# Decode attention on one core: the maximum of a head crosses partitions by two small TensorE products and two VectorE instructions instead of twelve VectorE instructions, and TensorE runs nine unread products meanwhile

## The chip, the cores and the metric

One core of one Trainium2 chip. The metric is device time in microseconds.

## The reference

Two attention blocks decode one token each, and their outputs are concatenated. A has 32 heads and 32 caches of 32768 keys; B has 32 heads over 8 caches, and only the last 4096 keys count. Head size is 128 and everything is bf16.

```python
# A, cut; B is the same on the last 4096 keys, four query heads to a cache
q = (x @ wq) ...                                     # 32 heads x 128
scores = einsum("bhqd,bhkd->bhqk", q, k_cache) * 128 ** -0.5
p = softmax(scores)
o = einsum("bhqk,bhkd->bhqd", p, v_cache)
return o.reshape(1, 1, 4096) @ wo
```

A's K and V are 8.39 MB each for a head, 16.78 MB together. That is what the kernel mostly does: read 570 MB once.

## The kernel before

A head of A goes like this. K (8.39 MB) and V (8.39 MB) arrive by two DMAs from one queue, in order: K of head g, V of head g, K of head g+1. The K tiles are transposed on TensorE (`psT`), copied out by VectorE (`kt`), and multiplied with the query into `psS`, 128 rows of 512 scores. Then come the maximum, the exponential on ScalarE, four transposes of the probabilities (`psPT`), and 64 products with V into `psACC` (called PV below). VectorE folds them, and TensorE gathers them into `psG`. The loop body holds two heads, and 16 trips make 32 heads.

The maximum, which the change touches. VectorE alone brings the row maxima of 128 partitions to one number and back:

```python
        o = dve(lambda v: v.reduce_max(tr["in"][:, 0:1], self.S[:, :], axis=AXX), self.sdone, self.k_pool)
        o = dve(lambda v: v.transpose(tr["a"][:, :], tr["in"][:, :]), o)
        for c in range(STRIPS):
            x = dve(lambda v, c=c: v.tensor_copy(m4[0:1, W * c:W * c + W], tr["a"][32 * c:32 * c + 1, 0:W]), o)
        o = dve(lambda v: v.reduce_max(t["mr"][0:1, :], m4[0:1, 0:4 * W].rearrange("p (k h) -> p h k", h=HG), axis=AXX), x)
        for c in range(STRIPS):
            x = dve(lambda v, c=c: v.tensor_copy(
                t["b"][32 * c:32 * c + 1, 0:W].rearrange("p (k h) -> p k h", k=KC),
                t["mr"][0:1, :].unsqueeze(1).to_broadcast([1, KC, HG])), o)
        o = dve(lambda v: v.transpose(t["cm"][:, :], t["b"][:, :]), x)
        o = dve(lambda v: v.tensor_scalar_mul(t["nb"][:, k:k + 1], t["cm"][:, 0:1], -self.SCALE), o, to="act")
        self.sread = self.op("act", lambda s: s.activation(
            out=self.psb[:, :], in_=self.S[:, :], func=ACTF.Exp, bias=t["nb"][:, k:k + 1], scale=self.SCALE,
            accum_out=t["oc"][k][:, DH:DH + 1]), o, self.psread, to="pe")
```

When buffers come free. V has one buffer, so the next V load is issued when PV of this head has ended. The next K load is issued when this head's transposes have left one part of the K buffer:

```python
    def load_v(self, g):
        self.load(self.vbuf[:, :], self.kv_src("v", "A", g)[:, 0, :], self.mark("v", 0), *self.free["v"])
    ...
        for g in range(NQH):
            self.loop = {"pe": g // 2, "dve": g // 2}
            self.load_k(g, 1 if g < NQH - 1 else 2)
            self.load_v(g)
            self.emit_qcopy(g)
            self.emit_unit("A", g)
            self.emit_stats("A", g)
            self.emit_PT("A", g)
            self.emit_PV("A", g)
```

The end. After the last head, both output matrices (`wo`) come in through the same queue, B's in two pieces and A's in four (12, 10, 6 and 4 of 32 row blocks). TensorE multiplies them as they land:

```python
    WO_CUTS = {"A": (0, 12, 22, 28, 32), "B": (0, 16, 32)}
    ...
    def emit_proj(self):

        for part in range(len(self.WO_CUTS["B"]) - 1):
            o = self.proj_part("B", part, lambda a: (self.S[32 * (a % 4):32 * (a % 4) + 1, :], (0, 32 * (a % 4)), a < 4, a >= 28))
        strips = self.op("dve", lambda v: v.tensor_copy(self.pb[:, :], self.S[:, :]), o)
        for part in range(len(self.WO_CUTS["A"]) - 1):
            last = self.proj_part("A", part, lambda a: (self.PT[0:1, :], None, a == 0, a == 31))
            if part == 0:
                o = self.op("pe", lambda e: e.matmul(self.ACC[0:1, :], lhsT=self.e32[:, 0:1], rhs=self.pb[:, :],
                                                     start=True, stop=True, skip_group_check=True), strips, self.accread)
                self.store("B", self.ACC, 512, o)
        self.store("A", self.PT, 0, last)
```

## Time and profile before

| | before |
|---|---|
| median of the first 3 runs | 1331.03 us (1330.01 to 1332.43) |
| span of the profiled run | 1330.5 us |
| bytes read | 570.4 MB |
| K of one head to K of the next | 38.7 us |
| start of the maximum to the exponential | 3.11 us |
| the 64 PV products of one head | 5.7 us |

From the page of the profile before: busy times, the granted TensorE clock and the DMA share in 40 slices (a digit is tenths), the load queue, and the chain of waits by engine.

```profile
span 1330.5 us, 28787 instructions
...
PE 953.2 (72%) x13274; PEld 668.9 (50%) x13274; DVE 805.0 (61%) x1661; ACT 54.8 (4%) x167; POOL 2.0 (0%) x15
...
PEclk9868788887788888778889878888987888888788
DMA  9999999999999999999999999999999999999997
...
q1 hardware_dynamic: 12628, 570.43, 99.4%
...
DMA 68%; PE 28%; DVE 3%; issue 0%; ACT 0%; SPq 0%
```

The transfer row stands at 9 throughout and the load queue is busy 99.4% of the span: the loads pace the program. The clock row dips in most slices, because TensorE pauses several times in each head.

One head in the timeline of before (start in us, duration in us, engine, line, operation; in brackets the idle time before and what ended it). The lines are the maximum, the exponential, PV, the issue of the next V load, and the first transposes of the next K.

```profile
610.83 0.69 DVE L522 TENSOR_REDUCE tr_in<-psS 128x1 f32<-128x512 f32 x1 [0.51 <-PE psS L505]
...
613.94 0.69 ACT L533 ACTIVATE psb<-psS,nb_A 128x512 bf16<-128x512 f32 x1 [35.86 <-DVE nb_A L532]
...
616.07 5.68 PE L571 MATMUL psACC<-vbuf,ptsb 128*4 128x512 bf16 x64 [0.69 <-ACT ptsb L546]
...
621.80 0.33 SPq L284 DMA_DIRECT2D vbuf<-in_A_v_cache_dram  x1
...
627.49 5.17 PE L483 MATMUL psT<-ident,kbuf 128*128 128x128 bf16 x64 [3.67 <-DMA kbuf<-in_A_k_cache_dram]
```

Read from top to bottom: 3.11 us from maximum to exponential, PV of 5.68 us, the next V issued at 621.80, and TensorE idle until K lands at 627.49.

The end of before: PV of head 31, B's 32 products, A's first 12, A's last 20, and the last eviction (the copy of A's result out of the accumulator).

```profile
1308.15 6.09 PE L571 MATMUL psACC<-vbuf,ptsb 128*4 128x512 bf16 x64 [0.69 <-ACT ptsb L546]
...
1317.15 3.29 PE L627 MATMUL psS<-kbuf,oz_B 128*1 128x512 bf16 x32
...
1320.27 2.75 PE L627 MATMUL psPT<-kbuf,oz_A 128*1 128x512 bf16 x12
...
1323.71 4.48 PE L627 MATMUL psPT<-kbuf,oz_A 128*1 128x512 bf16 x20
...
1328.23 0.68 DVE L633 CAST out_sb<-psPT 1x512 bf16<-1x512 f32 x1 [3.64 <-PE psPT L627]
```

No bracket here names a DMA. From K of head 30 on (first used at 1247.5 us), the program moves by computing alone.

### The profile page before, as it was taken

Reading aid. Unit: us, or ns where it says so; the run is one execution under the profiler, and the core shown is the slowest. Engines: PE = TensorE matmul, PEld = TensorE weight load, DVE = VectorE, ACT = ScalarE, POOL = GpSimd, SP = SyncE. Lnnn points to the kernel's source line nnn. Section 1 sums busy time; section 2 is a strip of 40 time slices with the busy share of each in tenths; the row PEclk is TensorE's granted clock in tenths of the full one; section 3 lists DMA queues with packets and bytes.
Section 4 is the critical chain, followed back from the end, with each engine's and each line's share of the span. In section 5 each row is a group of like instructions: output and inputs, shape, how many; then the busy total and the mean of one; then the engine's idle time right before and its main releaser. Section 6 shows DMA issues by size and latency. Waiting matters only on the chain.

```text
span 1330.5 us, 28787 instructions
## 1 busy us (share of the span) xinstructions
PE 953.2 (72%) x13274; PEld 668.9 (50%) x13274; DVE 805.0 (61%) x1661; ACT 54.8 (4%) x167; POOL 2.0 (0%) x15
## 2 busy tenths in 40 slices
PE   3756677686767778676687867668787667868777
PEld 3544445554444555444455544446554444555452
DVE  2655566765556676555667655566765556676573
ACT  0000000000000000000000000000000000000000
POOL 0000000000000000000000000000000000000000
PEclk9868788887788888778889878888987888888788
DMA  9999999999999999999999999999999999999997
GB/s 394 429 438 429 437 428 439 431 422 439 418 435 433 437 428 431 431 439 431 433 430 439 431 433 430 439 431 433 432 437 430 435 431 428 439 435 431 428 435 322
DMA packets 12932, 570.66 MB, mean 429 GB/s; under 512 B 1522, under 2 KB 1524, under 8 KB 1780
## 3 DMA queue, kind: packets, MB, share of 16 engines
q1 hardware_dynamic: 12628, 570.43, 99.4%
q8 instruction: 12, 0.20, 0.1%
q10 hardware_dynamic: 288, 0.00, 0.0%
q14 instruction: 4, 0.03, 0.0%
HBM read 570.43 MB, written 0.00 MB: 429 GB/s over the span
## 4 chain that ended last, share of the span: by engine, by line
DMA 68%; PE 28%; DVE 3%; issue 0%; ACT 0%; SPq 0%
DMA kbuf<-in_A_k_cache_dram 65%; PE psT L483 23%; PE psS L505 3%; DMA kbuf<-in_B_k_cache_dram 3%; DVE kt L486 3%; PE psACC L571 1%; PE psPT L627 1%; PE psS L627 0%; DVE oc_A L587 0%; ACT psb L533 0%; PE psPT L543 0%; DVE tr_in L522 0%; DVE b_A L528 0%; DVE m L525 0%; SPq L284 0%
## 5 line engine op out<-in xcount | busy, mean ns | idle before, releaser
L486 DVE COPY kt<-psT 128x1024 bf16<-128x1024 bf16 x1056 | 655.3, 684 | 203.0 <-PE psT L483 201.4
L483 PE MATMUL psT<-ident,kbuf 128*128 128x128 bf16 x8448 | 577.7, 234 | 135.8 <-DMA kbuf<-in_A_k_cache_dram 123.8
L483 PEld LDWEIGHTS psT<-ident,kbuf 128*128 128x128 bf16 x8448 | 538.3, 106 | 227.8 <-DMA kbuf<-in_A_k_cache_dram 131.9
L571 PE MATMUL psACC<-vbuf,ptsb 128*4 128x512 bf16 (+1 forms) x2112 | 188.5, 534 | 22.8 <-ACT ptsb L546 22.0
L505 PE MATMUL psS<-kt,qw 128*32 128x512 bf16 x2048 | 157.6, 385 | 15.5 <-DVE kt L486 15.5
L585 DVE TENSOR_SCALAR oc_A<-psACC,hot_A 128x128 f32<-128x128 f32 x32 | 11.2, 351 | 255.5 <-PE psG L598 255.5
L571 PEld LDWEIGHTS psACC<-vbuf,ptsb 128*4 128x4 bf16 (+1 forms) x2112 | 60.8, 111 | 141.9 <-issue 96.1
L543 PE MATMUL psPT<-ident,psb 128*128 128x128 bf16 x136 | 20.5, 305 | 127.9 <-ACT psb L533 127.9
L543 PEld LDWEIGHTS psPT<-ident,psb 128*128 128x128 bf16 x136 | 11.7, 130 | 137.6 <-ACT psb L533 137.4
L533 ACT ACTIVATE psb<-psS,nb_A 128x512 bf16<-128x512 f32 x32 | 22.0, 687 | 1169.7 <-DVE nb_A L532 1169.7
L505 PEld LDWEIGHTS psS<-kt,qw 128*32 128x32 bf16 x2048 | 34.0, 95 | 58.0 <-DVE kt L486 31.4
L598 PE MATMUL psG<-oc_A,hw 128*32 128x128 f32 (+1 forms) x128 | 19.3, 227 | 52.3 <-DVE oc_A L587 52.3
L598 PEld LDWEIGHTS psG<-oc_A,hw 128*32 128x32 f32 x128 | 11.4, 109 | 62.4 <-DVE oc_A L587 55.0
L587 DVE SCALAR_TENSOR_TENSOR oc_A<-psACC,hot_A,oc_A 128x128 f32<-128x128 f32 x96 | 33.7, 351 | 3.4
L522 DVE TENSOR_REDUCE tr_in<-psS 128x1 f32<-128x512 f32 x34 | 23.5, 692 | 17.1 <-PE psS L505 17.1
L525 DVE COPY m<-tr_a 1x16 f32<-1x16 f32 (+1 forms) x136 | 22.3, 164 | 2.6
L528 DVE COPY b_A<-mr_A 1x16 f32<-1x16 f32 x128 | 21.1, 165 | 2.4
L546 ACT ACTIVATE ptsb<-psPT 128x512 bf16<-128x512 bf16 x34 | 20.3, 597 | 32.3 <-PE psPT L543 32.3
L439 PE MATMUL psACC<-x_B,vbuf 128*128 128x1 bf16 x128 | 3.6, 165 | 13.4 <-DMA x_B<-in_B_x_dram 13.4
L439 PEld LDWEIGHTS psACC<-x_B,vbuf 128*128 128x128 bf16 x128 | 3.5, 104 | 13.4 <-DMA x_B<-in_B_x_dram 13.4
L446 DVE CAST qz<-psACC 128x32 bf16<-128x32 f32 x1 | 0.2, 192 | 12.9 <-PE psACC L439 12.9
L523 DVE STREAM_TRANSPOSE tr_a<-tr_in 128x32 f32<-128x32 f32 x34 | 7.2, 212 | 1.2
(66 smaller groups left out, 87.5 us busy)
## 6 DMA issues: line engine op xcount, KB each, us to landing
kbuf<-in_B_k_cache_dram SPq DMA_DIRECT2D x2, 4096.0 KB, 32.7
vbuf<-in_B_v_cache_dram SPq DMA_DIRECT2D x2, 4096.0 KB, 23.7
kbuf<-in_A_k_cache_dram SPq DMA_DIRECT2D x2, 4096.0 KB, 22.7
vbuf<-in_B_wq_dram SPq DMA_DIRECT2D x1, 4096.0 KB, 12.3
vbuf<-in_A_wq_dram SPq DMA_DIRECT2D x1, 4096.0 KB, 32.5
kbuf<-in_B_wo_dram SPq DMA_DIRECT2D x2, 2048.0 KB, 31.8
kbuf<-in_A_wo_dram SPq DMA_DIRECT2D x1, 1536.0 KB, 27.5
kbuf<-in_A_wo_dram SPq DMA_DIRECT2D x1, 1280.0 KB, 30.2
```

The costliest lines, as they stand in the source:

```text
L483: inst = e.transpose(T[:, 128 * k:128 * k + 128], src[:, DH * k:DH * k + DH], self.ident[:, :])
L486: self.copies.append(self.op("dve", lambda v: v.tensor_copy(KT[:, :], T[:, :]), o, to="pe"))
L505: inst = e.matmul(self.S[32 * c:32 * c + 32, :], lhsT=win, rhs=self.kt[(bb + c // 2) % NKT][:, 512 * (c % 2):512 * (c % 2) + 512], start=b ...
L522: o = dve(lambda v: v.reduce_max(tr["in"][:, 0:1], self.S[:, :], axis=AXX), self.sdone, self.k_pool)
L525: x = dve(lambda v, c=c: v.tensor_copy(m4[0:1, W * c:W * c + W], tr["a"][32 * c:32 * c + 1, 0:W]), o)
L528: x = dve(lambda v, c=c: v.tensor_copy(t["b"][32 * c:32 * c + 1, 0:W].rearrange("p (k h) -> p k h", k=KC), t["mr"][0:1, :].unsqueeze(1).to ...
L533: self.sread = self.op("act", lambda s: s.activation(out=self.psb[:, :], in_=self.S[:, :], func=ACTF.Exp, bias=t["nb"][:, k:k + 1], scale= ...
L543: inst = e.transpose(PT[:, 128 * jj:128 * jj + 128], self.psb[:, 128 * jj:128 * jj + 128], self.ident[:, :])
L546: self.ptread = self.op("act", lambda s: s.activation(out=self.ptsb[:, :], in_=PT[:, 0:512], func=ACTF.Copy), self.psread, to="pe")
L571: inst = e.matmul(acc[32 * c:32 * c + rows, 0:512], lhsT=lhsT, rhs=rhs, start=begin, stop=end, tile_position=(0, 32 * c), skip_group_check ...
L587: o = self.op("dve", lambda v, src=src, hot=hot: v.scalar_tensor_tensor(out=oc, in0=src, scalar=hot, in1=oc, op0=ALU.mult, op1=ALU.add), p ...
L598: return self.op("pe", lambda e: e.matmul(self.G[0:32, c0 + c:c0 + c2], lhsT=win, rhs=t["oc"][g % 2][:, c:c2], start=False, stop=True, ski ...
```

## The change

The intent is to shorten the path from scores to probabilities. After the first maximum, twelve small VectorE instructions become two products and two VectorE instructions. A product with the maxima as stationary operand lays them out along a row (`rows64` picks the right 16 of each strip), VectorE takes one maximum over 64, and a second product with a row of `-SCALE` spreads the scaled negative to 128 partitions. Nine products whose result nobody reads (`keep_busy`) are put between, so that the TensorE clock does not drop before PV. B keeps the old way.

```diff
--- before.py
+++ after.py
@@ -240,6 +240,8 @@
         self.e32 = sb("e32", [128, 32], F32)
         self.spread = sb("spread", [32, 4, 128], BF16)
         self.tr = {k: sb(f"tr_{k}", [128, 32], F32) for k in ("in", "a")}
+        self.rows64 = sb("rows64", [128, 64], F32)
+        self.nscale = sb("nscale", [1, 128], F32)
         self.m4 = sb("m4", [1, 128], F32)
         self.pb = sb("pb", [128, 512], F32)
         self.out_sb = sb("out_sb", [1, 1024], BF16)
@@ -403,6 +405,8 @@
         pool(lambda g: g.memset(self.tr["in"][:, :], 0.0))
         pool(lambda g: g.memset(self.qw[:, :], 0.0))
         pool(lambda g: g.memset(self.spread[:, :, :], 0.0))
+        pool(lambda g: g.memset(self.rows64[:, :], 0.0))
+        pool(lambda g: g.memset(self.nscale[:, :], -self.SCALE))
         for n in ("B", "A"):
             pool(lambda g, n=n: g.memset(c[n]["hsel"][:, :], 0.0))
             self.k_pool = pool(lambda g, n=n: g.memset(c[n]["b"][:, :], 0.0))
@@ -424,6 +428,10 @@
             lh = dve(lambda v, t=t, HG=HG, KC=KC: v.reduce_sum(
                 t["lh"][:, :], self.e32[:, 0:KC * HG].rearrange("p (k h) -> p h k", k=KC), axis=AXX), last)
             dve(lambda v, t=t, HG=HG: v.tensor_copy(t["hsel"][:, 32:32 + HG], t["lh"][:, :]), lh, self.k_pool)
+        for s in range(STRIPS):
+            rows = slice(32 * s, 32 * s + 32)
+            dve(lambda v, rows=rows, s=s: v.tensor_copy(self.rows64[rows, 16 * s:16 * s + 16],
+                                                        self.ident[rows, 32 * s:32 * s + 16]), self.k_pool)
         for dq in range(4):
             self.k_sel = dve(lambda v, dq=dq: v.tensor_copy(self.spread[:, dq, dq:128:4], self.ident[0:32, 0:32]),
                              self.k_pool)
@@ -519,7 +527,24 @@
         k = g % 2
         tr, m4 = self.tr, self.m4
         dve = lambda fn, *deps, **k: self.op("dve", fn, *deps, **k)
-        o = dve(lambda v: v.reduce_max(tr["in"][:, 0:1], self.S[:, :], axis=AXX), self.sdone, self.k_pool)
+        o = dve(lambda v: v.reduce_max(tr["in"][:, 0:1], self.S[:, :], axis=AXX), self.sdone, self.k_pool,
+                to="pe" if name == "A" else None)
+        if name == "A":
+
+            self.keep_busy(4)
+            o = self.op("pe", lambda e: e.matmul(self.ACC[0:1, 0:64], lhsT=tr["in"][:, 0:1], rhs=self.rows64[:, :],
+                                                 start=True, stop=True, skip_group_check=True),
+                        o, self.accread, self.k_sel, to="dve")
+            o = dve(lambda v: v.reduce_max(t["mr"][0:1, :], self.ACC[0:1, 0:64], axis=AXX), o, to="pe")
+            self.keep_busy(1)
+            o = self.op("pe", lambda e: e.matmul(self.ACC[:, 64:65], lhsT=self.nscale[:, :], rhs=t["mr"][0:1, :],
+                                                 start=True, stop=True, skip_group_check=True), o, to="dve")
+            self.keep_busy(4)
+            o = dve(lambda v: v.tensor_copy(t["nb"][:, k:k + 1], self.ACC[:, 64:65]), o, to="act")
+            self.sread = self.op("act", lambda s: s.activation(
+                out=self.psb[:, :], in_=self.S[:, :], func=ACTF.Exp, bias=t["nb"][:, k:k + 1], scale=self.SCALE,
+                accum_out=t["oc"][k][:, DH:DH + 1]), o, self.psread, to="pe")
+            return
         o = dve(lambda v: v.transpose(tr["a"][:, :], tr["in"][:, :]), o)
         for c in range(STRIPS):
             x = dve(lambda v, c=c: v.tensor_copy(m4[0:1, W * c:W * c + W], tr["a"][32 * c:32 * c + 1, 0:W]), o)
@@ -533,6 +558,16 @@
         self.sread = self.op("act", lambda s: s.activation(
             out=self.psb[:, :], in_=self.S[:, :], func=ACTF.Exp, bias=t["nb"][:, k:k + 1], scale=self.SCALE,
             accum_out=t["oc"][k][:, DH:DH + 1]), o, self.psread, to="pe")
+
+    def keep_busy(self, n):
+
+        def mm(e):
+            inst = None
+            for _ in range(n):
+                inst = e.matmul(self.PT[:, :], lhsT=self.ident[:, :], rhs=self.kt[0][:, 0:512], start=True, stop=True,
+                                skip_group_check=True)
+            return inst
+        self.op("pe", mm, self.ptread)
 
     def emit_PT(self, name, g):
         d, t = self.X[name], self.c[name]
```

## The prediction

> **What bounds the kernel now.** The loads. On the page, the transfer row of the 40 slices reads 9 everywhere but in the last, and the load queue is busy 99.4% of the span. 570.4 MB have to be read. In the middle, successive K tiles are first used at 588.8, 627.5, 666.2 and 704.9 us (chain of waits): 38.7 us for 16.78 MB, 434 GB/s. The Trainium skill, "DMA: Bandwidth & Descriptors", Specifications, gives a fabric ceiling of 435 GB/s; this trace agrees. The chain of waits is 68% DMA, 28% TensorE, 3% VectorE. The timeline of one head (600 to 640 us): TensorE ends at 623.8 and sits until 627.5, when the next K lands. The V load is issued at 621.8 but the K ahead of it lands only at 627.5, so it already queues 5.7 us; the K load issued at 637.9 lies some 9 us behind the V. The engine with slack is the computing side.
>
> **What the change does, per head of A (estimates from the timeline).** Now, from the start of the maximum over the scores (610.83) to the exponential (613.94) is 3.11 us: 0.69 maximum, then eleven small VectorE instructions of 0.15 to 0.21. Afterwards: 0.69, a product (0.27 with handoff, as the gather to the VectorE step at 621.6 shows), a maximum over 64 (0.25), a second product (0.27), a copy (0.2), and about 0.1 to 0.2 of delay from the unread products: about 1.9 us, so 1.2 us saved. VectorE loses some 1.8 us of work per head.
>
> The nine unread products cost about 2 us of TensorE (0.216 each at full clock) in time in which it is idle now (4.0 us before the transposes of the probabilities). They should keep the clock up: now it reads 0.50 from about 614 to 620, after that idle, and the 64 PV products take 5.7 us. The Trainium skill, "TensorE: Matmul & The Clock Gate", Part 1, puts the drop after an idle window of about 3.4 us; the trace agrees (two such drops per head). Warm, PV should take about 3.5 us. V is then released some 3 to 3.5 us earlier per head.
>
> **How much is on the critical path.** In 30 of 32 heads nothing: earlier release only lengthens the queue, and the TensorE wait for K grows from 4 to about 7 us. The tail is different. From 1247.5 us on, the chain is TensorE and VectorE: heads 30 and 31, then the output projections to 1328.2. There 3.5 us twice would be saved, but V of head 31 lands at 1305.6 (issue 1280.6 + 25.0) and the last piece of wo at about 1325.3 (1292.9 + 32.4), against the last product's end at 1328.2. Four products and the store remain, so at most about 2 us come off. With TensorE waiting for wo pieces in short bursts, its clock may fall and the 32 products run at 0.43 us: that could eat the gain. I expect 0.8 us.
>
> **Predicted: 1330.2 us, range 1328.2 to 1332.0.** Faster by over 2%: 0.01; within 2%: 0.98; slower by over 2%: 0.01.
>
> **Signs.** Right: the 38.7 us period and 434 GB/s unchanged; maximum to exponential about 1.9 us; the clock at 1.0 through PV, PV about 3.5 us; V issued 3 us earlier but landing at the same time, so time from issue to landing grows from 25 to about 28 us; VectorE busy down from 805 to about 747 us. Wrong: idle stretches in the transfer row, or the K period changing.
>
> **What would make it wrong.** Transfers slowing under the added reads; a hidden gap in the loads that the earlier release fills; the clock falling in the final projection, giving slightly slower; scatter between runs, which is 2.4 us in three runs already.

## The result

| | before | after |
|---|---|---|
| median, 6 runs each | 1331.85 us (1330.01 to 1332.43) | 1332.55 us (1330.07 to 1332.94) |
| ratio after / before | | 1.0004, 95% interval 0.9991 to 1.0017 |
| start of maximum to exponential | 3.11 us | 2.03 us |
| 64 PV products, mid-kernel head | 5.68 us | 3.63 us |
| VectorE busy | 805.0 us | 750.5 us |
| K of head 30 to the last eviction | 80.7 us | 82.4 us |

A ratio is the mean time of one kernel's fast runs over that of the other's in the same rounds, so it is not quite the ratio of the medians quoted.

The time did not move by an amount these runs can tell. The median of 1332.55 us lies above the predicted range (1328.2 to 1332.0). The page after, same lines as before:

```profile
span 1330.8 us, 29273 instructions
...
PE 969.7 (73%) x13658; PEld 690.4 (52%) x13690; DVE 750.5 (56%) x1345; ACT 54.8 (4%) x167; POOL 2.3 (0%) x17
...
PEclk9868899888889988888998888899888889988898
DMA  9999999999999999999999999999999999999996
...
q1 hardware_dynamic: 12628, 570.43, 99.3%
...
DMA 70%; PE 28%; DVE 1%; issue 0%; ACT 0%; SPq 0%
```

VectorE is relieved and the mean clock rose from 0.843 to 0.881 over the span, yet the transfers are as full as ever. One head of the changed kernel, the same five events:

```profile
610.50 0.69 DVE L530 TENSOR_REDUCE tr_in<-psS 128x1 f32<-128x512 f32 x1 [0.51 <-PE psS L513]
...
612.53 0.69 ACT L544 ACTIVATE psb<-psS,nb_A 128x512 bf16<-128x512 f32 x1 [37.71 <-DVE nb_A L543]
...
614.45 3.63 PE L606 MATMUL psACC<-vbuf,ptsb 128*4 128x512 bf16 x64 [0.69 <-ACT ptsb L581]
...
618.12 0.33 SPq L286 DMA_DIRECT2D vbuf<-in_A_v_cache_dram  x1
...
626.82 5.51 PE L491 MATMUL psT<-ident,kbuf 128*128 128x128 bf16 x64 [6.67 <-DMA kbuf<-in_A_k_cache_dram]
```

Every step is faster: 2.03 us from maximum to exponential, PV in 3.63 us, V issued 8.7 us before K is used, not 5.7. All of it turns into a longer wait for K, 6.67 us instead of 3.67. The end of the changed kernel: PV of head 31, B's products in two pieces, A's first 12, A's last 20, the last eviction.

```profile
1304.36 3.63 PE L606 MATMUL psACC<-vbuf,ptsb 128*4 128x512 bf16 x64 [2.25 <-DMA vbuf<-in_A_v_cache_dram]
...
1310.86 1.03 PE L662 MATMUL psS<-kbuf,oz_B 128*1 128x512 bf16 x16
...
1314.05 1.87 PE L662 MATMUL psS<-kbuf,oz_B 128*1 128x512 bf16 x16 [2.16 <-DMA kbuf<-in_B_wo_dram]
...
1317.76 5.28 PE L662 MATMUL psPT<-kbuf,oz_A 128*1 128x512 bf16 x12 [1.84 <-DMA kbuf<-in_A_wo_dram]
...
1324.01 4.48 PE L662 MATMUL psPT<-kbuf,oz_A 128*1 128x512 bf16 x20
...
1328.53 0.68 DVE L668 CAST out_sb<-psPT 1x512 bf16<-1x512 f32 x1 [3.64 <-PE psPT L662]
```

Head 31 reaches PV 3.8 us earlier and ends it over 6 us earlier (1308.0 against 1314.2; 1.4 us of that is an earlier K). But now the brackets name DMAs: TensorE waits for V, then for each piece of wo. A's first 12 products take 5.28 us where they took 2.75. Windows of the same stretch after (length, busy time of each engine, granted clock, DMA share, GB/s):

```profile
core 0: us, PE busy (x) PEld busy (x) DVE busy (x) ACT busy (x) POOL busy (x), PEclk, DMA share, GB/s
...
1312.00:1316.00 4.00, 1.87 (x16) 0.38 (x16) 0.02 (x1) 0.00 (x0) 0.00 (x0) 0.65 1.00 415
1316.00:1320.00 4.00, 2.24 (x6) 0.72 (x7) 0.67 (x1) 0.00 (x0) 0.00 (x0) 0.50 1.00 417
1320.00:1324.00 4.00, 4.00 (x10) 0.97 (x8) 0.00 (x0) 0.00 (x0) 0.00 (x0) 0.57 0.38 153
1324.00:1328.00 4.00, 4.00 (x20) 1.60 (x19) 0.68 (x1) 0.00 (x0) 0.00 (x0) 1.00 0.00 0
```

The packed traces hold only clock readings of 0.50 and 1.00, so a mean between them is a window in which the clock changed: 0.65 puts the drop at about 1313.2 and 0.57 the rise at about 1323.4. The clock is at half through all of A's first 12 products. It fell 1.3 us into a wait of only 2.16 us; in the 3.4 us before the drop TensorE had worked for about 1.5 us, in short pieces. The last eviction starts at 1328.53, no earlier than before's 1328.23, though K of head 30 had come 1.4 us earlier in this trace (1246.1).

### The profile page after: what moved, and what is told of

Read it like the earlier page. It is cut to its first block, busy times and chain, and to the rows that moved or that the text cites. A ratio compares the mean times of both kernels' runs of the same rounds, so it can differ in the third digit from the quotient of the medians.

```text
span 1330.8 us, 29273 instructions
## 1 busy us (share of the span) xinstructions
PE 969.7 (73%) x13658; PEld 690.4 (52%) x13690; DVE 750.5 (56%) x1345; ACT 54.8 (4%) x167; POOL 2.3 (0%) x17
## 3 DMA queue, kind: packets, MB, share of 16 engines
q1 hardware_dynamic: 12628, 570.43, 99.3%
## 4 chain that ended last, share of the span: by engine, by line
DMA 70%; PE 28%; DVE 1%; issue 0%; ACT 0%; SPq 0%
DMA kbuf<-in_A_k_cache_dram 64%; PE psT L491 23%; PE psS L513 4%; DMA kbuf<-in_B_k_cache_dram 3%; DMA kbuf<-in_A_wo_dram 2%; DVE kt L494 1%; PE psPT L662 1%; PE psACC L606 0%; SPq L286 0%; PE psACC L680 0%; PE psPT L567 0%; DVE oc_A L622 0%; ACT psb L544 0%; DVE out_sb L668 0%; PE psPT L578 0%
## 5 line engine op out<-in xcount | busy, mean ns | idle before, releaser
L606 PE MATMUL psACC<-vbuf,ptsb 128*4 128x512 bf16 (+1 forms) x2112 | 121.6, 383 | 24.3 <-ACT ptsb L581 21.3
L606 PEld LDWEIGHTS psACC<-vbuf,ptsb 128*4 128x4 bf16 (+1 forms) x2112 | 48.5, 87 | 85.9 <-ACT ptsb L581 26.7
L567 PE MATMUL psPT<-kt,ident 128*128 128x512 bf16 x256 | 71.6, 382 | 5.1 <-issue 5.1
L567 PEld LDWEIGHTS psPT<-kt,ident 128*128 128x128 bf16 x288 | 22.9, 97 | 26.7 <-issue 7.3
L578 PEld LDWEIGHTS psPT<-ident,psb 128*128 128x128 bf16 x136 | 7.8, 99 | 18.9 <-ACT psb L544 18.7
L578 PE MATMUL psPT<-ident,psb 128*128 128x128 bf16 x136 | 13.7, 224 | 3.0
L538 DVE TENSOR_REDUCE mr_A<-psACC 1x1 f32<-1x64 f32 x32 | 6.8, 212 | 14.9 <-PE psACC L535 14.9
L540 PEld LDWEIGHTS psACC<-mr_A,nscale 1*128 1x128 f32 x64 | 9.4, 182 | 8.9 <-DVE mr_A L538 8.9
L543 DVE COPY nb_A<-psACC 128x1 f32<-128x1 f32 x32 | 5.1, 158 | 15.0 <-PE psACC L540 15.0
```

The source lines that it names most:

```text
L567: inst = e.matmul(self.PT[:, :], lhsT=self.ident[:, :], rhs=self.kt[0][:, 0:512], start=True, stop=True, skip_group_check=True)
L578: inst = e.transpose(PT[:, 128 * jj:128 * jj + 128], self.psb[:, 128 * jj:128 * jj + 128], self.ident[:, :])
L606: inst = e.matmul(acc[32 * c:32 * c + rows, 0:512], lhsT=lhsT, rhs=rhs, start=begin, stop=end, tile_position=(0, 32 * c), skip_group_check ...
```

## The experiments

Four questions: is the difference real, what took the gain of the tail back, which part of the change did what, and how much slack the 30 steady heads have. Besides the ratios I use one number from each trace, from the first use of K of head 30 to the start of the last eviction. It leaves out whatever the loads did earlier.

### before_again: before against itself

No edit.

> The kernel before, unchanged, timed against itself: the ratio should be 1.000, and shows how far apart two equal kernels come out. Its trace is a second look at the end: I expect the last V to be used at about 1308, the last product to end at about 1328 and the store 2.3 us later, all within 1.5 us of the first profile.

Measured: ratio 0.9998 (0.9985 to 1.0012), median 1331.47 us. K of head 30 at 1246.4 us, the last eviction at 1326.71: 80.3 us. PV began at 1306.7 and the last products ended at 1326.7, both 1.5 us before the first profile's, the edge of what I allowed. Two traces of one kernel thus differ by 1.1 us before the tail even starts.

### after_again and after_third: the changed kernel again

No edit.

> The changed kernel, unchanged. Theory 1 (the tail is won and then lost: head 31 ends 6 us earlier, but TensorE then waits in pieces for wo and its clock falls, so the first 12 products of the last projection take 5.3 us and not 2.6): same time as before within 1.5 us, with the clock at 0.50 when those 12 products start. Rival 2 (the last landing of wo alone sets the end): the same time too, but then the last 20 products would wait for a DMA. Rival 3 (only scatter: there was a gain of 0.8 us, hidden): the ratio to before comes out at 0.9994 or less.

> The changed kernel a third time, in the same rounds as the version with the repaired tail. Theory 1: 81 to 82.5 us from K of head 30 to the last product, ratio to before between 0.9985 and 1.0015.

Measured: ratios 0.9998 (0.9983 to 1.0012) and 1.0002 (0.9989 to 1.0016), medians 1331.76 and 1331.48 us; 81.3 and 81.0 us from K of head 30, the third at the lower edge of what was expected. A's first 12 products took 4.44 and 4.15 us, and no DMA stands in front of the last 20. One detail of the expectation was missed: in after_again the clock still read 1.00 when these products started (1317.87) and fell at about 1318.3, half a us into them. Over all 17 runs of the changed kernel the mean is 1331.8 us; over all 55 runs of before it is 1331.7 (standard deviations 0.9 and 1.1 us). The groups were not all taken on one chip, so this is a check and not a ratio. It excludes no gain of a few tenths, but it gives the forecast of 0.8 us no support.

### after_warm_tail: keep the clock up in the final projection

```diff
         for part in range(len(self.WO_CUTS["B"]) - 1):
             o = self.proj_part("B", part, ...)
+            self.keep_busy(8 if part == 0 else 12)
```

> The changed kernel, with 8 and 12 more unread products in the two waits of TensorE for pieces of wo in the final projection. Theory 1: the clock stays at 1.0, the 12 products take 2.6 us, the last product ends about 2.5 to 3 us earlier, the time falls by 2 to 3 us against the changed kernel (ratio to before about 0.998). Rival 2 (the last landing sets the end): no change, below 0.5 us.

Measured: ratio 0.9991 (0.9978 to 1.0005), 0.7 thousandths below the changed kernel of the same rounds, about 0.9 us; 80.5 us from K of head 30. Its timeline (PV of head 31, the 12 unread products, A's first 12, the last eviction):

```profile
1304.30 4.96 PE L606 MATMUL psACC<-vbuf,ptsb 128*4 128x512 bf16 x64 [3.55 <-DMA vbuf<-in_A_v_cache_dram]
...
1315.90 2.76 PE L567 MATMUL psPT<-kt,ident 128*128 128x512 bf16 x12
...
1318.59 2.75 PE L662 MATMUL psPT<-kbuf,oz_A 128*1 128x512 bf16 x12
...
1326.56 0.68 DVE L668 CAST out_sb<-psPT 1x512 bf16<-1x512 f32 x1 [3.64 <-PE psPT L662]
```

The clock is repaired: 2.75 us for the 12 products. But the unread products hold the array until 1318.6, while the first piece of wo was in use from 1317.5 to 1317.9 in the traces of the changed kernel, and the late, cold PV (4.96 us, after a wait of 3.55 us for V) had pushed the row back first. So the mechanism holds and the size of 2 to 3 us does not. Rival 2, that only the landing of wo counts, does not fit: the end moved, while V of head 31 came into use 58.2 us after K of head 30 here as in all three traces of the changed kernel.

### before_warm_tail: the same aid for the kernel before

```diff
         pv = self.emit_gather(name, g, DH, DH + 1)
+        if name == "A":
+            self.keep_busy(7)
...
+        self.keep_busy(2)
         self.emit_spread("A")
```

> The kernel before, with 7 unread products in every head of A while VectorE folds the PV sums, and 2 before the last normalisation. Theory 1: the 32 strip products of B's projection run warm and take 1.8 us, not 3.3, so the last product ends about 1.3 us earlier and the time falls by about 1 us; the steady heads do not move (K period 38.7 us). Rival 2: no change, since wo lands no earlier.

Measured: ratio 0.9988 (0.9975 to 1.0002), median 1330.52 us, and 80.6 us from K of head 30. B's 32 products ran warm (1.90 us against 3.29), as expected. But head 31 began its maximum 56.1 us after K of head 30, against 55.4 and 55.0 in the two traces of before. The seven unread products did not hold the gather up: it follows the issue of the V load of head 31 by 1.6 us here as there. Head 30 was late before its own seven (its probabilities were transposed 26.4 us after its K, against 26.0 and 25.6) and its PV was longer (5.93 us against 5.69 and 5.67); why was not tested. The median is about as forecast, but the interval contains 1 and the trace's tail is not shorter, so it is open whether these runs are quicker by more than noise, and why.

### products_only, twice, and unread_only: which half does what

```diff
# products_only: the changed kernel without its unread products
-            self.keep_busy(4)
...
-            self.keep_busy(1)
...
-            self.keep_busy(4)
# unread_only: the kernel before, after the copy that ends the maximum
         o = dve(lambda v: v.tensor_scalar_mul(t["nb"]..., -self.SCALE), o, to="act")
+        if name == "A":
+            self.keep_busy(15)
```

> The two small products without the nine unread ones. If shortening the maximum and holding the clock are separate effects: maximum to exponential 1.9 us as in the changed kernel (from 3.1), but the 64 PV products stay near 5 us, between 3.6 and 5.9, because TensorE still idles for over 2 us before them. K period unchanged at 38.7 us; the whole within 1.5 us of before. If it were the products that keep the clock up, PV would be 3.6 us here too.

> The maximum on VectorE as before, with 15 unread products while it runs. Maximum to exponential 3.1 us as before; the 64 PV products 3.6 us, the clock at 1.0. K period 38.7 us; whole time within 1.5 us of before. That would make the clock, not the maximum, the larger part (2.1 of 3.4 us) of what a head gained.

> The two products without unread ones, again. Its end came 79.6 us after K of head 30, since the 32 strip products of B ran in one cold piece of 3.4 us just before A's, which then ran at full clock. If that follows from the order of the waits and not from chance: 79.3 to 80 us again, time 0.5 to 1 us under before. If it hangs on where the clock's windows fall: anything from 79.5 to 82.

Measured, products alone: maximum to exponential 1.93 us, PV 5.17 and 4.85 us in two neighbouring heads. Unread products alone: 3.12 us, PV 3.63 us in both. The two halves are separate, as expected: the products shorten the chain by 1.1 to 1.2 us, and the unread ones hold the clock, which is worth 2.1 us of PV. In the head of products_only that starts its maximum at 610.7 us, no wait of TensorE between scores and PV is longer than 1.06 us, and yet the clock falls to half at about 613.7: no single long wait was needed. The ratios are 0.9995 (0.9978 to 1.0012) and 1.0001 (0.9985 to 1.0018): neither half moves the time.

The tail of unread_only is 81.3 us, with A's first 12 products at 4.43 us. The tail of products_only came out at 79.6 us, the shortest so far. Its lines are B's 32 products, A's first 12, the last eviction:

```profile
1313.76 3.40 PE L659 MATMUL psS<-kbuf,oz_B 128*1 128x512 bf16 x32
...
1317.95 2.75 PE L659 MATMUL psPT<-kbuf,oz_A 128*1 128x512 bf16 x12 [0.80 <-DMA kbuf<-in_A_wo_dram]
...
1325.91 0.68 DVE L665 CAST out_sb<-psPT 1x512 bf16<-1x512 f32 x1 [3.64 <-PE psPT L659]
```

And the same kernel again, at 81.2 us, with B's products in two pieces:

```profile
1312.20 1.03 PE L659 MATMUL psS<-kbuf,oz_B 128*1 128x512 bf16 x16
...
1313.87 1.03 PE L659 MATMUL psS<-kbuf,oz_B 128*1 128x512 bf16 x16 [0.64 <-DMA kbuf<-in_B_wo_dram]
...
1317.56 4.41 PE L659 MATMUL psPT<-kbuf,oz_A 128*1 128x512 bf16 x12 [2.65 <-DMA kbuf<-in_A_wo_dram]
...
1327.18 0.68 DVE L665 CAST out_sb<-psPT 1x512 bf16<-1x512 f32 x1 [3.64 <-PE psPT L659]
```

The same program ran A's 12 products in 2.75 us once and in 4.41 us once. In the first trace B's products ran in one piece of 3.40 us right before; in the second TensorE waited for both pieces and then 2.65 us for A's. The second reading in the expectation is the right one: where the clock stands at the end varies between runs of one program. This pair is also the cleanest test of what the clock costs: the first piece of A's wo came into use 71.6 us after K of head 30 in both traces, and the 1.66 us between the two times of the 12 products are the 1.65 us between the two tails. The repeat's ratio was 0.9995 (0.9981 to 1.0008).

### change_body_only and change_tail_only: where the change acts

```diff
-            self.loop = {"pe": g // 2, "dve": g // 2}
+            self.loop = {"pe": g // 2, "dve": g // 2} if g < NQH - 2 else {}
...
-        if name == "A":
+        if name == "A" and g < NQH - 2:       # tail only: g >= NQH - 2
```

> The change in heads 0 to 29 alone, heads 30 and 31 as before (unrolled). Theory 1 (the loads set the pace of the body, and only the tail can move): from the landing of K of head 30 to the end of the last product about 80.5 us as in the two traces of before, K period 38.7 us, same time as before. A rival in which the body gains or loses time shows it as another K period: 0.05 us more or less per head would be 1.5 us.

> The change in heads 30 and 31 alone. Theory 1: from the landing of K of head 30 to the end of the last product 81 to 82.5 us, as in the two traces of the changed kernel (82.4 and 81.3) and longer than before's 80.3 to 80.7, although head 31 ends some 5 us earlier; 12 products of the last projection take 4 to 5.3 us. Rival 2 (the landing of wo sets the end): 79 us.

Measured: 0.9999 (0.9982 to 1.0016) and 1.0009 (0.9993 to 1.0026); tails of 81.1 us both. The period was 38.7 us in the body as expected. But change_body_only missed 80.5 us, and change_tail_only ran A's first 12 products in 2.75 us, not 4 to 5.3. Something disturbed both: the first piece of A's wo was waited for until 73.2 us after K of head 30, where the looped changed kernel has it at 71.6 us. Each had 18 instruction packets and not 12. But delay_2us below, unrolled with 18 packets as well, has that piece at 71.6 us, so unrolling alone is not shown to be the cause. The two runs do not settle where the change acts.

### best: a repair that unrolled the end

```diff
# on the changed kernel; the loop again ends before head 30
+        if name == "A" and g == NQH - 1:
+            self.keep_busy(10, self.T[1], self.copies[-1])      # before PV of head 31
...
+            self.keep_busy(6 if part == 0 else 3)               # after each piece of B
...
+        o = self.op("pe", ... ACC[0:1, :] ... strips ...)        # B's row sum, moved ahead of A's products
+        self.store("B", self.ACC, 512, o)
+        self.keep_busy(3)
```

> The changed kernel with a tail that stays warm and is not held up: heads 30 and 31 unrolled, 10 unread products while head 31 waits for V, 6, 3 and 3 in the waits of the last projection, and B's row sum moved ahead of A's products. The last piece of wo lands 77.8 us after K of head 30 (both profiles), and 4 products of 0.22 us follow, so the floor is 78.7 us. Theory 1: the last product ends 78.7 to 79.5 us after K of head 30, against 80.3 to 80.7 before and 81.3 to 82.4 in the changed kernel; the time falls by about 1.5 us against before and 2.5 us against the changed kernel. If the clock did not matter: no difference to after_warm_tail (80.5).

Measured: 0.9998 (0.9984 to 1.0011), 80.8 us. It missed: A's first 12 products started at 1319.7 us, 73.4 us after K of head 30, because wo again landed late (their first weight load waits for it). The name was premature. Its five runs lie within 0.15 us (1330.89 to 1331.04), where nine runs of before in the same rounds span 2.8 us; no experiment says why.

### tail_repaired: the same without unrolling

```diff
# as above, but the loop is left as it was, and in every head:
+        if name == "A":
+            self.keep_busy(8, self.T[1], self.copies[-1])
...
+            self.keep_busy(5 if part == 0 else 3)
```

> The changed kernel, loop not unrolled, with 8 unread products in every head between the transposes of the probabilities and PV (they bridge the wait of head 31 for V), 5, 3 and 3 in the waits of the last projection, and B's row sum moved ahead of A's products. If the clock in the last projection is all that took the gain: the 12 products take 2.6 to 2.8 us, the last product ends 79 to 79.7 us after K of head 30 (floor 78.7), the time is 1.5 us under before's and 2 us under the changed kernel's, and the runs scatter less than before's 0.9 us. If wo lands later again or the end is over 80.3: the clock is not all.

Measured: 0.9991 (0.9977 to 1.0005), median 1330.90 us; 79.2 us from K of head 30. PV of head 31, A's first 12, A's last 20, the last eviction:

```profile
1305.33 3.63 PE L607 MATMUL psACC<-vbuf,ptsb 128*4 128x512 bf16 x64
...
1317.58 2.75 PE L665 MATMUL psPT<-kbuf,oz_A 128*1 128x512 bf16 x12
...
1320.69 4.48 PE L665 MATMUL psPT<-kbuf,oz_A 128*1 128x512 bf16 x20 [0.36 <-DMA kbuf<-in_A_wo_dram]
1325.20 0.68 DVE L671 CAST out_sb<-psPT 1x512 bf16<-1x512 f32 x1 [7.65 <-PE psPT L665]
```

PV is warm though V was waited for, the 12 products take 2.75 us, and the first of the last 20 waits for its piece of wo. This is 1.1 to 1.5 us under before's tail and 1.8 to 3.2 us under the changed kernel's. That is the gain that a better ordered end could have had. The ratio agrees in size (1.2 us) but its interval contains 1, and the forecast of less scatter failed (1329.5 to 1332.1). It is the shortest tail among the versions meant to be faster, and not proven faster than before by total time.

Side by side, the tails of the looped versions add up (us; the start and the tail count from the first use of K of head 30):

| trace | A's first 12 start | they take | from their end to the last eviction | tail |
|---|---|---|---|---|
| before | 72.75 | 2.75 | 5.21 | 80.71 |
| before_again | 72.34 | 2.75 | 5.21 | 80.30 |
| after | 71.64 | 5.28 | 5.49 | 82.41 |
| after_again | 71.60 | 4.44 | 5.21 | 81.25 |
| after_third | 71.61 | 4.15 | 5.22 | 80.98 |
| products_only | 71.62 | 2.75 | 5.21 | 79.58 |
| products_only_again | 71.61 | 4.41 | 5.21 | 81.23 |
| after_warm_tail | 72.52 | 2.75 | 5.22 | 80.49 |
| tail_repaired | 71.61 | 2.75 | 4.87 | 79.23 |

The first piece of A's wo comes into use at 71.6 us at the earliest, so of all that head 31 gains only 0.7 to 1.2 us reach A's first product. The half-rate clock then costs 1.4 to 2.5 us. With the clock at full rate and the old order the tail is 79.6 us (products_only); the new order is worth another 0.35 us.

### slack_24 and slack_48: a test of the body's slack that went astray

```diff
# changed kernel, loop ends before head 30
         self.gath = self.emit_gather(name, g, 0, DH)
+        if name == "A" and self.loop:
+            self.keep_busy(24)                # slack_48: 48
```

> The changed kernel with 24 more unread products at the end of each of heads 0 to 29, 5.2 us of TensorE. If the steady heads have the slack I read (TensorE waits 6.7 us for K, and the next V load is issued 8.7 us before the K ahead of it lands), nothing moves: K period 38.7 us, time within 1.5 us of the changed kernel, the wait for K down to about 1.5 us or less. If computing or the release of buffers set the pace anywhere in the body, the time rises by a good part of 30 times 5.2 us = 156 us.

> The same with 48, 10.4 us. A head then computes for 32.0 + 10.4 us, less about 1.7 us since the transposes start warm: 40.7 us, over the 38.7 us of the loads. I expect a period of 40 to 41 us and 40 to 70 us more in all, no TensorE wait for K, and gaps in the transfers. If the time does not rise, the slack is larger than I read.

Measured: +24 us (ratio 1.0183, 1.0167 to 1.0198) and +152 us (44.0 us a head, not 40 to 41). Neither was forecast. TensorE in slack_24 still waited for K (4.9 us in the head I looked at), and V was issued 7.1 to 13.0 us before the K ahead of it was used, so it was no lack of slack in computing. Its queues:

```profile
q1 hardware_dynamic: 12628, 570.43, 98.2%
q8 instruction: 145, 2.38, 0.7%
```

All versions with a looped tail above have 12 instruction packets and 0.20 MB. With 48 more products in a trip, instructions were fetched 145 times, 2.38 MB. Many periods alternate near 40.2 and 38.7 us, and 1.5 us for each of the 15 trips would be 22.5 of the 24 us; in every trace of the table further below the period from head 1 to head 2, where the loop begins to repeat, is 39.9 to 40.2 us too. That the fetch causes it fits but was not isolated. As a test of slack this was void.

### delay_2us and delay_8us: delaying the head by VectorE instead

```diff
# kernel before, loop ends before head 30
+        if name == "A" and self.loop:
+            for _ in range(3):                # delay_8us: 12
+                o = dve(lambda v: v.tensor_copy(self.pb[:, :], self.S[:, :]), o)
         o = dve(lambda v: v.tensor_scalar_mul(t["nb"]..., -self.SCALE), o, to="act")
```

> The kernel before with three more VectorE copies of 0.69 us ahead of the exponential in heads 0 to 29 (30 and 31 unrolled), so each such head and its V release come 2.1 us later. The wait for K is 3.7 us and the V load is issued 5.7 us before the K ahead of it lands: nothing should move, K period 38.7 us, time within 2 us of before (the unrolled heads may cost up to 1.6). If the body had no slack: 60 us more.

> The same with twelve copies, 8.3 us. That is 4.6 us beyond the wait for K: period about 43 us, 110 to 145 us more in all, no TensorE wait for K left.

Measured: +14 us (ratio 1.0110, 1.0094 to 1.0125) and +116 us (1.0870). The second is in the forecast span, with 42.6 us a head where about 43 was expected. The first refutes what I had read: 2.1 us should have fitted into a slack of 3.7 to 5.7. Lines of delay_2us: the issue of a V load, the first use of the K ahead of it, and of the next K.

```profile
628.88 0.33 SPq L284 DMA_DIRECT2D vbuf<-in_A_v_cache_dram  x1
...
632.84 3.82 PE L483 MATMUL psT<-ident,kbuf 128*128 128x128 bf16 x64 [1.95 <-DMA kbuf<-in_A_k_cache_dram]
...
672.11 5.28 PE L483 MATMUL psT<-ident,kbuf 128*128 128x128 bf16 x64 [3.57 <-DMA kbuf<-in_A_k_cache_dram]
```

TensorE still waits for K, 1.95 us, so it is not computing that binds. The V load was issued 3.96 us before K was used, and the next K came after 39.3 us, not 38.7. Head by head the link is plain. Of the 28 V loads for heads 2 to 29, 13 were issued under 4 us before the K ahead of them was used, and 12 of these were followed by a period over 38.95 us (mean 39.55); 9 were issued 4.5 us or more before, and one of these was (mean 38.8). Note that the load queue still reads 99.3% busy in this run, though it moved its bytes at 425 and not 429 GB/s over the span: that share alone does not show that no time is lost.

### after_delay_2us: the same delay on the changed kernel

```diff
# changed kernel, loop ends before head 30
+            if self.loop:
+                for _ in range(3):
+                    o = dve(lambda v: v.tensor_copy(self.pb[:, :], self.S[:, :]), o)
             o = dve(lambda v: v.tensor_copy(t["nb"]..., self.ACC[:, 64:65]), o, to="act")
```

> The changed kernel with the same three VectorE copies (2.1 us) ahead of the exponential in heads 0 to 29, heads 30 and 31 unrolled as in delay_2us. If the lead of the V load over the landing of the K ahead of it is what counts, and about 4.4 us of it are needed: the lead falls from 9.0 to about 7 us (5 if the clock drops in the longer wait), all periods but the first stay at 38.7 us, and the time is within 2 us of before (delay_2us: 14 us more). If any delay of a head costs time: about 14 us more here too.

Measured: 1.0013 (0.9996 to 1.0030), median 1333.44 against 1331.10: 2.3 us, where before lost 14. The clock did drop in the longer wait (PV 4.9 to 5.3 us), so the lead fell to 5.4 us, and 8 of 30 periods are over 38.95. The forecast that all periods stay is thus missed, though the profiled run (1337.0 us) was 3.6 us or more above the three others (1332.3 to 1333.5) and overstates it; delay_2us was profiled in its quickest run (1342.7). The delay cost a small part of what it cost before. Head by head the link to the lead is looser here: from head 2 on, 7 periods are over 38.95 us, and 5 of them follow a lead under 5 us. From the traces, the 30 periods from head 0 to head 30, lead = from the issue of a V load to the use of the K ahead of it:

| trace | mean lead, us | mean period, us | periods over 38.95 us |
|---|---|---|---|
| after (three traces) | 9.0 | 38.75 | 1, 1, 2 |
| tail_repaired | 7.2 | 38.76 | 1 |
| before (two traces) | 5.8, 5.7 | 38.80, 38.77 | 3, 1 |
| after_delay_2us | 5.4 | 38.89 | 8 |
| delay_2us | 4.2 | 39.18 | 17 |

The mean includes the one long period from head 1 to head 2. The kernel before stands at the edge: in the first trace its shortest lead is 4.4 us, and a period of 39.2 us follows it. What the change bought in the body is distance from that edge, and almost none of it is time.

## Why the prediction was right or wrong

- *The loads bind.* Right: queue busy 99.4 and 99.3%, 38.7 us a period in both.
- *Maximum to exponential about 1.9 us, PV about 3.5 us, VectorE 747 us.* Right: 2.03, 3.63 and 750.5 us. The two halves act apart, as products_only and unread_only show.
- *In 30 of 32 heads nothing is gained.* Right in the time: mean periods of 38.75 to 38.80 us in all five traces of the two kernels. The reason given, that V "already queues 5.7 us", read a lead as a slack. delay_2us shows that 2.1 us off that lead costs 14 us.
- *At most 2 us can come off the end.* Supported: the repaired tail is 1.1 to 1.5 us shorter than before's.
- *"I expect 0.8 us."* This is the step that failed. It is the term for the clock in the final projection, of which the prediction said that it "could eat the gain", and for which it in effect left 1.2 of the 2 us. The mechanism was right, its size was not. In three traces the clock took more than all: A's first 12 products ran 5.28, 4.44 and 4.15 us and not 2.75, a loss of 1.4 to 2.5 us, and the tail came out at 81.0 to 82.4 us against 80.3 and 80.7. The bound of 2 us was loose as well: the prediction looked at the last piece of wo, but the wait for the first piece lets A's products start only 0.7 to 1.2 us earlier, so 2 us were not there to be had in this order. With the clock held and B's row sum moved forward the tail is 79.2 us.
- *1328.2 to 1332.0.* The miss of 2.35 us (1332.55 less 1330.2) is made of three parts: 0.83 us of gain that did not come (1331.03 less 1330.2), 0.82 us since before's median of three runs was low (1331.85 with six), and 0.70 us between the medians in the same runs, which is within the interval of the ratio. The later medians of the changed kernel, 1331.76 and 1331.48, lie inside the range, so that the first one fell outside is in part chance. The range was too narrow for a baseline of three runs that already spread over 2.4 us.

Shown: the tail's gain existed, and the half-rate clock in the last products was the cause of its loss: in the table above, with A's first piece of wo at 71.6 us and the order unchanged, the tails differ by what the clock did to the products, and by nothing else over 0.05 us (in the trace of after, 0.3 us of it fall on B's row sum, which ran 1.34 us there and 1.02 us elsewhere). Holding the clock alone brought the end from 81.0 to 82.4 us down to 80.5; holding it through the wait for V too, in a better fitted row and with B's row sum moved forward, brought 79.2, of which the order is 0.35 us. These are single traces. Not shown: by total time, that any version beats before; the intervals of all versions meant to be faster contain 1.

The Trainium skill, "TensorE: Matmul & The Clock Gate", part 1, explains why the clock varies: its window of about 3.4 us runs freely and is not tied to the program's start. The traces agree: in all of them every full stretch of one clock is a whole multiple of 3.41 us (10.24 us for the half-rate one at the end of after), and one program had A's first 12 products at 2.75 us in one run and at 4.41 us in another.

## What to carry to other kernels

When an engine off the critical path is made faster, ask what it will then wait for, and in what state it comes out of that wait. Here a TensorE that was ahead of its loads worked in short bursts at half clock, and lost at the end what it had gained. And a load that is issued 5.7 us before the one ahead of it lands is not 5.7 us of slack: delay it and measure.

## What the Trainium skill lacked or had wrong

- "TensorE: Matmul & The Clock Gate", "Why this matters for your kernels", advises to avoid idle gaps of over about 3 us. Here the clock also fell in waits of 2.16 us and, in products_only, of at most 1.06 us between short pieces of work. Nor does it say that unread products which fill a gap can themselves be late: 12 of them ran 0.9 us past the time at which the piece of wo that they bridged is in use elsewhere, and took back part of their gain (80.5 us against 79.6 in products_only with the same order).
- The same page, Part 4, says that transposes do not count as TensorE activity for the full clock. In the trace of before the clock rose from 0.50 (628 to 630 us) to 0.87 on average (630 to 632) while TensorE ran nothing but 128x128 transposes through the identity; the first score products came at 632.6. Whether these use the mode the page means is not shown here.
- "DMA: Bandwidth & Descriptors" gives a ceiling of 435 GB/s, which fits (434), but not how far ahead the next load has to be issued to keep it: with 8.39 MB loads, mean leads of 5.7 us and more kept 38.8 us a head, 4.2 us gave 39.2. What makes up those us stays open.
- "Runtime: NRT & Kernel Launch", "Instruction fetch mechanics", calls the cost of crossing a block of instructions mostly hidden, and no page gives a time for such fetches beside a saturated load queue: 145 packets (2.38 MB) in place of 12 went with 24 us more. Cause not isolated. (18 in place of 12 went with the output weights 1.4 to 1.8 us later in five runs, and with no delay in delay_2us.)
